# Two decode attention blocks on one core: who issues the loads of x, and how the last cast is split

## The chip, the cores and the metric

The kernel runs on one core of a Trainium2 chip. A core has a matrix engine (TensorE, PE in the profile), two engines for elementwise work (VectorE, DVE; ScalarE, ACT), GpSimd (POOL) and SyncE (SP), which here only issues DMAs. Sixteen DMA engines move data between HBM and the core's SBUF; SyncE and ScalarE each issue into a queue of their own (q1 and q10 in the profile), and both queues run on the same sixteen engines. Engines run side by side and wait for each other and for DMAs by semaphores. TensorE's results land in PSUM, from which VectorE or ScalarE copies them. The metric is device time in microseconds (us) of one execution; the profile's span is the part of it between the first and the last event of the program's engines and DMAs.

## The reference

Two independent problems, A and B, of the same shape; their outputs are put side by side. Each is one decoding step of attention with 2 batches, 32 query heads, 16 key and value heads and a window of the last 4096 positions:

```python
q = (x @ wq).reshape(B, Sq, Hq, Dh)            # x: 2 x 1 x 576, wq: 576 x 4096
k = repeat(k_cache[:, :, Sk - W:, :], 2)       # W = 4096, Dh = 128
v = repeat(v_cache[:, :, Sk - W:, :], 2)
scores = einsum("bhqd,bhkd->bhqk", q, k) * Dh ** -0.5
o = einsum("bhqk,bhkd->bhqd", softmax(scores), v)
out = o.reshape(B, Sq, Hq * Dh) @ wo           # wo: 4096 x 576, out: 2 x 1 x 576
```

Everything is bfloat16. x is tiny (2 rows of 576 numbers, 1152 bytes a row), the weights and above all the cache windows are large: 153 MB are read in all.

## The kernel before, in words

The kernel first builds lists of operations, one list for each engine, in `_Sched` (`S.add(engine, function, dependencies, name)`), and then emits each list in its order with the semaphore waits that the dependencies need. `dma_op` adds a DMA issue to an engine's list. What stands earlier in an engine's list is issued earlier.

**The stream.** Large loads go through a ring of four slots of 4 MB each (`ring`). The list `stream` fixes their order: the query weights of A and of B ("Q"), then K and V windows of the slabs in turn, 16 slabs in all (8 for each problem, each of four key/value heads). SyncE issues them all. A load into a slot waits until the last reader of the slot's previous content is done (`reader`); for a K slab this is VectorE's transpose, for a V slab the matmul with the probabilities, for the query weights the last query matmul. `issue_slab` issues one slab, `issue_wq` the query weights of one problem: first the last 64 of the 576 rows, as 128 half rows of 4 KB (`wqr`, 512 KB), then the other 512 rows (4 MB) into a ring slot. The output weights wo go into a buffer `wob` of their own, in four parts placed between the slabs; the last problem's very last heads come in three small DMAs at the end of the stream (`issue_last`).

**The start.** `load_x` loads x of one problem: a DMA of two rows into `x_sb`. In the kernel before, x of A is the first thing that ScalarE's list holds, and x of B is issued by SyncE at the end of `issue_wq` for A, behind the 4 MB. VectorE meanwhile builds masks (`init_small`), then copies the tail of x (line 380, which waits for both x). TensorE transposes x with five small matmuls (line 375), ScalarE and VectorE cast the result into `xT` (lines 389 and 397), and the query projection begins (`do_qpair`, lines 450 and 188, the second being the helper that reuses loaded weights). It waits for `xT`, the 4 MB of its problem and the half rows of both problems. ScalarE takes the queries out of PSUM (lines 465 and 470), VectorE transposes them (475), ScalarE stores them (483).

**The loop.** For each slab VectorE transposes K in four pieces (line 515), TensorE computes scores (540), VectorE finds maxima (550), ScalarE exponentiates (585), VectorE transposes the probabilities (593), TensorE multiplies with V (631), ScalarE takes the result out (643), and GpSimd, TensorE and VectorE combine it. Groups of heads are then multiplied with wo (`do_proj`, line 786).

**The end.** The output has 576 columns, more than one PSUM bank of 512 float32 numbers. Through most of the kernel the first 512 columns sum up in the bank `OT` and the other 64 apart. Before the last heads, the sums of B are moved into two places of the scores' PSUM tensor, one in each of two banks, that `fin(0)` and `fin(1)` name: ScalarE copies columns 0 to `NH` (line 810), VectorE then adds the 64 (811) and copies the rest (813). The last heads' matmuls add to both (line 790), and `do_E` casts the two to the output row, ScalarE the first (822) and VectorE the second (823). SyncE then issues the output's DMA (831). `NH` is half of 576.

Of the kernel before, what the change touches and what calls it, by code (L numbers as in the profile page):

```python
# [8 lines left out]
ALU = mybir.AluOpType  # L9
# [50 lines left out]
def build_kernel(nc, probs, out, cfg=None):  # L60
# [8 lines left out]
    NPROB = len(probs)  # L69
    Bb, _one, D = x0.shape  # L70
# [12 lines left out]
    ND = SPP * NPROB  # L83
# [5 lines left out]
    HH = HD // 2  # L89
    NXC = NFC + 2  # L90
    NOUT = wo0.shape[1]
    NH = NOUT // 2
    NB0 = 512
    NB1 = NOUT - NB0
    assert NOUT % 2 == 0 and 0 < NB1 <= NB0
    SCALE = float(Dh) ** -0.5
    ZW = 152
    BIG = -1.0e30
# [8 lines left out]
    def by_group(G):  # L107
        return G < NG - 1

    def wo_slot(G):  # L110
        return {0: 0, 1: 8, 2: 16, 3: 24, 4: 0, 5: 8, 6: 16, 7: 24}[G]

    es = ExitStack()
    with es:
# [3 lines left out]
        wob = sb("wob", [128, NSW, NOUT], BF16)  # L118
# [46 lines left out]
        o_rest = sb("o_rest", [Bb, NB1], FP32)  # L165
# [6 lines left out]
        ST = [ps("st%d" % i, [128, 1024]) for i in range(2)]  # L172
# [13 lines left out]
        def matmul_again(e, first, out_ap, rhs, start, stop, skip=True):  # L186
            i = first.ins
            return e.add_instruction(mybir.InstMatmult(  # L188
                name=nc.get_next_instruction_name(), engine=i.engine, ins=[e.lower_ap(rhs), i.ins[1]], outs=[e.lower_ap(out_ap)],
                start_tensor_calc=start, stop_tensor_calc=stop, tile_size=i.tile_size, tile_position=i.tile_position,  # L190
                bass_skip_group_check=skip, ldweights=False))
# [4 lines left out]
        def dma_op(eng, sem_h, n_dmas, fn, deps, tag):  # L196
            op = S.add(eng, fn, deps, tag)
            dma_count[sem_h] = dma_count.get(sem_h, 0) + 16 * n_dmas
            op.dma = (sem_h, dma_count[sem_h])
            return op  # L200

        def load_x(P, eng):
            return dma_op(eng, x_sem, 1, lambda e: e.dma_start(
                x_sb[P * Bb:(P + 1) * Bb, :], probs[P][0][:, 0, :]).then_inc(x_sem, 16), [], "xload%d" % P)
        x_dma = {0: load_x(0, "act")}

        p_ones_b = S.add("pool", lambda e: e.memset(ones_b[:], 1.0), [], "ones_b")
        p_ident_b = S.add("pool", lambda e: e.affine_select(ident_b[:], ones_b[:], [[-1, 128]], ALU.is_equal, 0.0,
# [50 lines left out]
        def issue_wq(n, P):  # L259
            wqP = probs[P][3]  # L260
            r = n % NR
            deps = [reader[n - NR]] if n >= NR else []
            wq_dma[P] = dma_op("sp", wq_sem, 1, lambda e: e.dma_start(
                wqr[:, P, :], wqP[NFC * 128:D, :].rearrange("r (h n) -> r h n", h=2)).then_inc(wq_sem, 16), [], "wqr%d" % P)
            slab_dma[n] = dma_op("sp", ring_sem[r], 1, lambda e: e.dma_start(
                ring[:, r, :], wqP[0:NFC * 128, :].rearrange("(p s) n -> p (s n)", s=NFC)).then_inc(ring_sem[r], 16), deps, "wq%d" % P)

            if P == 0:
                for P_ in range(1, NPROB):
                    x_dma[P_] = load_x(P_, "sp")  # L270

        def issue_last(woP, lo, r0, deps):
            for n_, hs in enumerate(HEADS):
# [51 lines left out]
        rest_add = {}  # L325
# [7 lines left out]
        def tb_job(fn, tag, deps, which=None):  # L333
            n = tbn[0]
            tbn[0] += 1
            w = (tb_last[0] + 1) % NTB if which is None else which
            tb_last[0] = w
            bank = TB[w]
            d = list(deps)
            if tb_open[w] is not None:  # L340
                d.append(tb_open[w]())
            tb_open[w] = lambda: tb_consumer[n]
            return n, bank, S.add("pe", lambda e: fn(e, bank), d, tag)
# [417 lines left out]
        fin_ops = []  # L761

        def fin(half):
            return ST[(ND - 2) % 2][32 * half:32 * half + Bb, 512 * half:512 * half + NH]

        def do_proj(D_):
            G = D_ // 2
            P = G // GPP
            u = unit_of[G]
            s0 = 8 * (G - UNITS[u][0])  # L770
            w0 = wo_slot(G)
            new = G % GPP == 0
            if by_group(G):
                parts = [([(Rsb[u % 2][:, :, s0 + s_], s_) for s_ in range(8)], [r_ev[u], wo_dma[G]], new, True, True)]
            elif D_ < ND - 1:
                parts = [([(Rsb[u % 2][:, :, s_], s_) for s_ in range(4)], [r_ev[u], wo_dma[G]] + fin_ops, False, False, False)]
            else:
                parts = [([(oTn[:, h, :], 4 + h) for h in hs], [norm[D_], wo_last[n_]], False, False, n_ == len(HEADS) - 1)
                         for n_, hs in enumerate(HEADS)]
            for lhs, deps, start, rstart, rstop in parts:  # L780
                def f(e, rest, lhs=lhs, start=start, rstart=rstart, rstop=rstop):
                    last = None
                    for n_, (l_, s_) in enumerate(lhs):
                        begin, end = n_ == 0, n_ == len(lhs) - 1
                        if by_group(G):
                            first = e.matmul(OT[0:Bb, 0:NB0], l_, wob[:, w0 + s_, 0:NB0], start=start and begin, stop=end, skip_group_check=True)  # L786
                            last = matmul_again(e, first, rest[0:Bb, 0:NB1], wob[:, w0 + s_, NB0:NOUT], rstart and begin, rstop and end)
                        else:
                            for half in range(2):
                                last = e.matmul(fin(half), l_, wob[:, w0 + s_, half * NH:(half + 1) * NH],  # L790
                                                start=False, stop=end, skip_group_check=True)
                    return last
                deps = deps + [e_ops[(P - 1, 0)]]
                if by_group(G):
                    n, bank, proj[D_] = tb_job(f, "proj%d" % D_, deps)
                    rest_at[G] = bank
                    if G % GPP < GPP - 1 and G < NG - 2:
                        d = [proj[D_]]
                        if new:
                            if P:  # L800
                                d.append(e_ops[(P - 1, 1)])
                            rest_add[G] = S.add("dve", lambda e: e.tensor_copy(o_rest[:, :], bank[0:Bb, 0:NB1]), d, "rest%d" % G)
                        else:
                            d.append(rest_add[G - 1])
                            rest_add[G] = S.add("dve", lambda e: e.tensor_tensor(o_rest[:, :], o_rest[:, :], bank[0:Bb, 0:NB1], ALU.add),
                                                d, "rest%d" % G)
                        tb_consumer[n] = rest_add[G]
                    elif G == NG - 2:
                        d = [proj[D_], chain[(ND - 2, "exp")], chain[(ND - 2, "max")]]
                        a_ = S.add("act", lambda e: e.activation(fin(0), OT[0:Bb, 0:NH], ACTF.Copy), d, "fin0")  # L810
                        tb_consumer[n] = S.add("dve", lambda e: e.tensor_tensor(
                            fin(1)[:, NB0 - NH:NH], o_rest[:, :], bank[0:Bb, 0:NB1], ALU.add), d + [rest_add[G - 1]], "fin1")
                        fin_ops.append(S.add("dve", lambda e: e.tensor_copy(fin(1)[:, 0:NB0 - NH], OT[0:Bb, NH:NB0]), [a_], "fin2"))
                    else:
                        rest_at[G] = (n, bank)
                else:
                    proj[D_] = S.add("pe", lambda e, f=f: f(e, None), deps, "proj%d" % D_)

        def do_E(P):
            G = (P + 1) * GPP - 1  # L820
            if G == NG - 1:
                e_ops[(P, 0)] = S.add("act", lambda e: e.activation(out_sb[P][:, 0:NH], fin(0), ACTF.Copy), [proj[2 * G + 1]], "Elo%d" % P)
                e_ops[(P, 1)] = S.add("dve", lambda e: e.tensor_copy(out_sb[P][:, NH:NOUT], fin(1)), [proj[2 * G + 1]], "Ehi%d" % P)
# [25 lines left out]
        for s in range(ND):  # L849
# [31 lines left out]
            if s in proj_at:  # L881
                do_proj(2 * proj_at[s] + 1)
                if proj_at[s] == GPP - 1:
                    do_E(0)
# [20 lines left out]
        do_comb(D_)  # L905
        do_norm(D_)
        do_proj(2 * 5 + 1)
        do_redist(2)
        do_comb(ND - 2)
        do_norm(ND - 2)  # L910
        do_proj(D_)
        D_ = ND - 1
        issue_until(len(stream) - 1)
# [78 lines left out]
def bass_concat_heads__sliding_block_cached__sliding_block_cached__decode_kernel(  # L992
    nc, A_x, A_k_cache, A_v_cache, A_wq, A_wo, B_x, B_k_cache, B_v_cache, B_wq, B_wo, out,
):
    build_kernel(nc, [(A_x, A_k_cache, A_v_cache, A_wq, A_wo), (B_x, B_k_cache, B_v_cache, B_wq, B_wo)], out)
# [28 lines left out]
```

## Time and profile before

| what | before |
|---|---|
| device time, median of 3 runs | 362.7 us (362.63 to 363.06) |
| the profiled execution | 363.02 us |
| its span | 361.8 us |
| moved by DMA | 153.27 MB, mean 424 GB/s |
| TensorE, VectorE, ScalarE, GpSimd busy | 60%, 56%, 19%, 10% of the span |
| VectorE transposes of K (line 515) | 64 times, 2284 ns each, 145.3 us |
| last cast, ScalarE / VectorE | 0.400 / 0.449 us |

The profile comes from one execution; its engine rows give start, duration, engine, line, operation and what it wrote from what it read. A bracket at the end of a row gives the engine's idle time before it and what ended that idle time. A row with SPq or ACTq is a DMA issue: its duration is that of the issuing, not of the transfer. "To landing" is the time from issue to the semaphore update that says all data is there. The chain of waits goes back from the last event to what released it, step by step.

### The profile page before, as it was taken

To read this page: it belongs to the slowest core of one execution; us is meant where nothing else is said; L and a number is where in the kernel's file an instruction comes from. 1 tells how busy PE (TensorE), PEld (TensorE's weight loads), DVE (VectorE), ACT (ScalarE), POOL (GpSimd) and SP (SyncE) were. 2 spreads that over 40 slices of the span, in tenths; PEclk is the share of its full clock that TensorE was granted. 3 is DMA by queue.
4 is the path that set the end of the run, shared out by engine and by line. 5 is a ranking of instruction groups with operands and counts; after the bars stand their busy time and mean duration, and the time that the engine had idled before them with its cause. 6 is when DMAs were issued, how large, how long until landed. Compare 5 with 4: busy or idle time off the path is not lost.

```text
span 361.8 us, 2730 instructions
## 1 busy us (share of the span) xinstructions
PE 218.6 (60%) x1318; PEld 55.8 (15%) x945; DVE 200.9 (56%) x175; ACT 68.2 (19%) x149; POOL 35.3 (10%) x55
## 2 busy tenths in 40 slices
PE   0399195763747207466574737766867707657786
PEld 0010021120111101112120201212121201211132
DVE  4112599846647019283756658392919239079931
ACT  1036502130203002103020203020201203002131
POOL 1000000004000400001300040002100040200020
PEclk9999689997889857969698978899898978969999
DMA  8999999999999999999999999999999999999996
GB/s 348 421 449 406 464 406 437 431 408 453 415 442 438 428 424 438 429 428 438 417 446 422 435 428 442 426 435 428 424 424 440 431 424 433 431 438 428 438 409 248
DMA packets 6491, 153.27 MB, mean 424 GB/s; under 512 B 712, under 2 KB 1232, under 8 KB 1616
## 3 DMA queue, kind: packets, MB, share of 16 engines
q1 hardware_dynamic: 6476, 153.10, 98.8%
q8 instruction: 9, 0.15, 0.2%
q14 instruction: 2, 0.02, 0.0%
q10 hardware_dynamic: 4, 0.00, 0.0%
HBM read 153.10 MB, written 0.00 MB: 423 GB/s over the span
## 4 chain that ended last, share of the span: by engine, by line
DMA 72%; DVE 17%; PE 7%; ACT 3%; SPq 1%; issue 0%
DMA ring<-in_B_k_cache_dram 34%; DMA ring<-in_A_k_cache_dram 27%; DVE xt L515 14%; DMA wob<-in_B_wo_dram 8%; DMA wob<-in_B_x_dram 3%; PE st L188 3%; PE st L540 3%; ACT wob L465 1%; DVE wob L475 1%; ACT qk L483 1%; PE st L450 1%; DVE m L550 1%; ACT wob L470 1%; DVE nM L563 0%; SPq L252 0%
## 5 line engine op out<-in xcount | busy, mean ns | idle before, releaser
L515 DVE STREAM_TRANSPOSE xt<-ring 128x2048 f32<-128x2048 f32 x64 | 145.3, 2284 | 86.6 <-DMA ring<-in_A_k_cache_dram 49.8
L540 PE MATMUL st<-xt,zq 128*128 128x512 bf16 x256 | 111.6, 436 | 122.6 <-DVE xt L515 98.1
L188 PE MATMUL st<-xt,zq 128*128 128x512 bf16 x256 | 110.1, 430 | 0.0
L540 PEld LDWEIGHTS st<-xt,zq 128*128 128x128 bf16 x256 | 27.1, 106 | 216.3 <-DVE xt L515 113.5
L631 PE MATMUL acc<-ring,pC 128*32 128x512 bf16 x512 | 32.5, 381 | 1.2 <-DMA ring<-in_B_v_cache_dram 1.2
L568 ACT ACTIVATE nMrep<-nM 1x128 f32<-1x128 f32 x16 | 4.9, 308 | 146.9 <-DVE nM L563 146.9
L643 ACT ACTIVATE acc_sb<-acc 128x512 bf16<-128x512 f32 x16 | 9.5, 596 | 79.9 <-PE acc L631 79.9
L593 DVE STREAM_TRANSPOSE pC<-pR 128x1024 bf16<-128x1024 bf16 x16 | 19.6, 1223 | 3.7 <-ACT pR L585 2.1
L650 POOL TENSOR_TENSOR acc_sb<-acc_sb,masks 128x1024 bf16<-128x1024 bf16 (+1 forms) x8 | 13.4, 1679 | 66.6 <-ACT acc_sb L643 66.6
L550 DVE TENSOR_REDUCE m<-st 128x1 f32<-128x1024 f32 x16 | 19.0, 1190 | 1.4 <-PE st L188 1.4
L502 POOL TENSOR_TENSOR zq<-qk,masks 128x128 bf16<-128x128 bf16 x16 | 6.3, 398 | 136.2 <-PE st L188 114.4
L585 ACT ACTIVATE pR<-st,bias_sb 128x1024 bf16<-128x1024 f32 x16 | 17.8, 1114 | 0.5
L475 DVE STREAM_TRANSPOSE wob<-wob 128x512 f32<-128x512 f32 x8 | 5.7, 711 | 20.3 <-ACT wob L465 12.9
L415 ACT ACTIVATE st<-maskB 128x1024 f32<-128x1024 bf16 x16 | 16.5, 1032 | 1.6 <-POOL rsel L600 0.4
L786 PE MATMUL ot<-wob,Rsb 128*2 128x512 bf16 x56 | 15.2, 390 | 0.0
L631 PEld LDWEIGHTS acc<-ring,pC 128*32 128x32 bf16 x512 | 12.4, 96 | 15.9 <-issue 3.2
L600 POOL TENSOR_TENSOR rsel<-masks,rsum 128x16 f32<-128x16 bf16 x8 | 1.7, 216 | 108.0 <-ACT pR L585 108.0
L188 PE MATMUL tb<-wob,Rsb 128*2 128x64 bf16 x56 | 10.9, 195 | 0.0
L375 PE MATMUL tb<-wob 4*128 4x16 bf16 x5 | 0.3, 179 | 14.5 <-DVE wob L380 14.5
L653 POOL TENSOR_TENSOR acc_sb<-acc_sb 128x512 bf16<-128x512 bf16 (+1 forms) x8 | 8.2, 1029 | 0.6
L188 PE MATMUL st<-ring,wob 128*128 128x512 bf16 x24 | 7.9, 445 | 0.0
L579 ACT ACTIVATE bias_sb<-tb 128x1 f32<-128x1 f32 x16 | 2.7, 171 | 24.8 <-PE tb L573 24.8
(89 smaller groups left out, 99.5 us busy)
## 6 DMA issues: line engine op xcount, KB each, us to landing
ring<-in_A_k_cache_dram SPq DMA_DIRECT2D x8, 4096.0 KB, 30.4
ring<-in_A_v_cache_dram SPq DMA_DIRECT2D x8, 4096.0 KB, 32.5
ring<-in_B_k_cache_dram SPq DMA_DIRECT2D x8, 4096.0 KB, 28.4
ring<-in_B_v_cache_dram SPq DMA_DIRECT2D x7, 4096.0 KB, 32.8
wob<-in_A_wo_dram SPq DMA_DIRECT2D x1, 4608.0 KB, 43.3
ring<-in_A_wq_dram SPq DMA_DIRECT2D x1, 4096.0 KB, 12.7
ring<-in_B_wq_dram SPq DMA_DIRECT2D x1, 4096.0 KB, 22.6
ring<-in_B_v_cache_dram SPq DMA_DIRECT2D x1, 3072.0 KB, 25.5
```

The lines of the kernel that those rows point to most:

```text
L188: return e.add_instruction(mybir.InstMatmult(name=nc.get_next_instruction_name(), engine=i.engine, ins=[e.lower_ap(rhs), i.ins[1]], outs=[ ...
L415: chain[(s, "fill")] = S.add("act", lambda e: e.activation(ST[s % 2][:, :].rearrange("k (h j) -> k h j", h=2), maskB[:].unsqueeze(1).broad ...
L475: chain[(G, "qtr")] = S.add("dve", lambda e: e.transpose(qtr[:].bitcast(FP32), qrow[:].bitcast(FP32)), evs, "qtr%d" % G)
L515: Xop[(s, u)] = S.add("dve", lambda e: e.transpose(xt[:, i % NKT, :].rearrange("k (j w) -> k j w", w=64), ring[:, n % NR, :].bitcast(FP32) ...
L540: first = last = e.matmul(bank, zq[:, p4, s % NZQ, w0:w0 + 128], mv, start=False, stop=stop, skip_group_check=True)
L550: chain[(s, "max")] = S.add("dve", lambda e: e.tensor_reduce(m1[:, 0:1], ST[s % 2][:, :], AX.X, ALU.max), d, "max%d" % s)
L585: chain[(s, "exp")] = S.add("act", lambda e: e.activation(pR[:, :], ST[s % 2][:, :], ACTF.Exp, bias=bias_sb[:, 0:1], scale=SCALE, accum_ou ...
L593: chain[(s, "pC")] = S.add("dve", lambda e: e.transpose(pC[:, s % NPT, :, :].rearrange("k j c -> k (j c)"), pR[:, :]), d, "pC%d" % s)
L631: last = e.matmul(ACC[32 * cb:32 * cb + 32, 0:512], pC[:, D_ % NPT, j0_:j0_ + 4, :].rearrange("k j c -> k (j c)"), ring[:, n % NR, j0_ * 1 ...
L643: acc_ev[D_] = S.add("act", lambda e: e.activation(acc_sb[:, D_ % 2, :], ACC[:, :], ACTF.Copy), d, "accev%d" % D_)
L650: t = S.add("pool", lambda e: e.tensor_tensor(v, v, maskJ[:].unsqueeze(1).unsqueeze(3).broadcast_to([128, l1 - l0, 4, 128]), ALU.mult), [a ...
L786: first = e.matmul(OT[0:Bb, 0:NB0], l_, wob[:, w0 + s_, 0:NB0], start=start and begin, stop=end, skip_group_check=True)
```

## The change

Both loads of x are issued by SyncE, between the half rows (`wqr`) of A's query weights and their 4 MB; ScalarE issues none. Independently, `NH` goes from 288 to 320, so that ScalarE copies and casts 320 columns of the last output and VectorE 256; the matmuls of the last heads and the copies that preload `fin(0)` and `fin(1)` follow the new border.

```diff
-    NH = NOUT // 2
+    NH = NOUT * 5 // 9
     NB0 = 512
     NB1 = NOUT - NB0
...
-        x_dma = {0: load_x(0, "act")}
+        x_dma = {}
...
             wq_dma[P] = dma_op("sp", wq_sem, 1, lambda e: e.dma_start(
                 wqr[:, P, :], wqP[NFC * 128:D, :].rearrange("r (h n) -> r h n", h=2)).then_inc(wq_sem, 16), [], "wqr%d" % P)
+            if P == 0:
+                for P_ in range(NPROB):
+                    x_dma[P_] = load_x(P_, "sp")
             slab_dma[n] = dma_op("sp", ring_sem[r], 1, lambda e: e.dma_start(
                 ring[:, r, :], wqP[0:NFC * 128, :].rearrange("(p s) n -> p (s n)", s=NFC)).then_inc(ring_sem[r], 16), deps, "wq%d" % P)
-
-            if P == 0:
-                for P_ in range(1, NPROB):
-                    x_dma[P_] = load_x(P_, "sp")
...
-            return ST[(ND - 2) % 2][32 * half:32 * half + Bb, 512 * half:512 * half + NH]
+            return ST[(ND - 2) % 2][32 * half:32 * half + Bb, 512 * half:512 * half + (NOUT - NH if half else NH)]
...
-                                last = e.matmul(fin(half), l_, wob[:, w0 + s_, half * NH:(half + 1) * NH],
+                                last = e.matmul(fin(half), l_, wob[:, w0 + s_, half * NH:NOUT if half else NH],
...
-                            fin(1)[:, NB0 - NH:NH], o_rest[:, :], bank[0:Bb, 0:NB1], ALU.add), d + [rest_add[G - 1]], "fin1")
+                            fin(1)[:, NB0 - NH:NOUT - NH], o_rest[:, :], bank[0:Bb, 0:NB1], ALU.add), d + [rest_add[G - 1]], "fin1")
```

More of the change, by code (lines that the diff above doesn't have):

```diff
@@ L91, in build_kernel @@
     NOUT = wo0.shape[1]
-    NH = NOUT // 2
+    NH = NOUT * 5 // 9
     NB0 = 512
     NB1 = NOUT - NB0
-    assert NOUT % 2 == 0 and 0 < NB1 <= NB0
+    assert NOUT % 9 == 0 and 0 < NB1 <= NOUT - NH and NH < NB0
     SCALE = float(Dh) ** -0.5
```

## The prediction

> **What bounds the kernel now.** I read three views in this order: the page's slices, to see whether one resource is full throughout; the chain of waits, to see what sets the end; the timeline of the first and last microseconds, since the change touches only those. The slices and the queues come first.
>
> ```profile
> DMA  8999999999999999999999999999999999999996
> GB/s 348 421 449 406 464 406 437 431 408 453 415 442 438 428 424 438 429 428 438 417 446 422 435 428 442 426 435 428 424 424 440 431 424 433 431 438 428 438 409 248
> ...
> q1 hardware_dynamic: 6476, 153.10, 98.8%
> ...
> q10 hardware_dynamic: 4, 0.00, 0.0%
> ```
>
> Every slice but the first and the last has the 16 DMA engines at 90% or more, and SyncE's queue q1 alone fills 98.8% of the span. The kernel streams 153.10 MB and is bound by that stream; its time is the stream's start, plus its bytes, plus what follows the last byte. q10 is ScalarE's queue, with the four packets of x of problem A. The start, in the timeline (columns: start us, duration us, engine, line, what):
>
> ```profile
> 0.79 0.53 ACTq L203 DMA_DIRECT2D wob<-in_A_x_dram  x1
> 0.79 0.40 SPq L263 DMA_DIRECT2D wob<-in_A_wq_dram  x1
> ...
> 1.25 0.41 SPq L265 DMA_DIRECT2D ring<-in_A_wq_dram  x1
> ...
> 1.72 0.31 SPq L203 DMA_DIRECT2D wob<-in_B_x_dram  x1
> ...
> 14.20 0.21 DVE L380 COPY wob<-wob 4x128 bf16<-4x128 bf16 x1 [9.47 <-DMA wob<-in_B_x_dram]
> ...
> 15.42 0.59 PE L450 MATMUL st<-wob 128*128 128x512 bf16 x1 [0.63 <-DVE wob L397]
> ```
>
> VectorE waited 9.47 us for x of problem B, which queued behind 4 MB of wq; that looks like the prize. The end:
>
> ```profile
> 356.87 0.61 PE L631 MATMUL acc<-ring,pC 128*32 128x512 bf16 x8 [1.01 <-DMA ring<-in_B_v_cache_dram]
> ...
> 359.75 0.08 PEld L790 LDWEIGHTS st<-wob,oTn 128*2 128x2 bf16 x2 [0.27 <-DMA wob<-in_B_wo_dram]
> 360.08 0.40 ACT L822 ACTIVATE pR<-st 2x288 bf16<-2x288 f32 x1 [1.88 <-PE st L790]
> 360.08 0.45 DVE L823 CAST pR<-st 2x288 bf16<-2x288 f32 x1 [1.37 <-PE st L790]
> 360.57 0.26 SPq L831 DMA_DIRECT2D out_dram<-pR  x1
> ```
>
> The last wo rows land at 359.71 by the chain; then two matmuls (0.31 us), the two casts side by side, VectorE's the longer, and the output's DMA, with the span's end at 361.8.
>
> **The early x, as a gain.** Both x go out right behind the first wq half rows (512 KB). Those landed 3.5 us after their issue by the view of DMAs, at 4.29, so both x are there by about 4.4 (my estimate: the same landing and two tiny rows). VectorE is busy with masks until 4.72, so x's preparation (copy 0.21, matmuls 0.32, casts 0.22 and 0.19: the rows from 14.20 to 15.28, 1.1 us in all) ends near 5.8 instead of 15.28. The q projection has two other waits. The 4 MB of wq landed at 1.25 + 12.7 = 13.95, and the second problem's half rows, for which every projection also waits, at 2.07 + 13.2 = 15.27. So the first matmul of q moves from 15.42 to about 15.3: 0.1 us, not 9. Of the 9.47 us VectorE's wait loses, all is idle time of an engine off the path; what is late next is the second half rows.
>
> What that 0.1 us is worth: the q matmuls free the first two ring slots, and the next 4 MB loads go out at 26.99 and 36.04. The load of 36.04 took 29.02 us in the chain. 4 MB at the 437 GB/s of most 6 us stretches take 9.6 us, so it lay some 19 us behind earlier transfers. Loads issued 0.1 us earlier start no earlier. Gain: 0, from 0 to 0.1; the backlog of 19 us is the cover.
>
> **The early x, as a cost.** In SyncE's order the 4 MB come two issues later: x issues take 0.31 each on SyncE, with 0.06 between issues, so 2 x 0.37 = 0.74. The 4 MB issue moves from 1.25 to 1.99, the second half rows from 2.07 to 2.44 (one issue more than before), and the second 4 MB and the two K slabs by the same 0.37. Does the stream stall? The windows of a quarter microsecond show when data moves (columns: busy time by engine, then PE's clock, DMA share, GB/s; packets are counted where they start):
>
> ```profile
> 1.50:1.75 0.25, 0.00 (x0) 0.00 (x0) 0.22 (x1) 0.25 (x1) 0.00 (x0) 1.00 0.01 5
> 1.75:2.00 0.25, 0.00 (x0) 0.00 (x0) 0.20 (x1) 0.25 (x1) 0.00 (x0) 1.00 0.94 147
> ...
> 3.00:3.25 0.25, 0.00 (x0) 0.00 (x0) 0.25 (x2) 0.00 (x0) 0.00 (x0) 1.00 1.09 442
> 3.25:3.50 0.25, 0.00 (x0) 0.00 (x0) 0.25 (x2) 0.00 (x0) 0.00 (x0) 1.00 2.29 934
> ```
>
> The half rows, issued at 0.79, start to move at about 1.8: 1.0 us from issue to first packet. The jump to 934 GB/s between 3.25 and 3.50 is the first big packets of the 4 MB. By the same 1.0 us they could have moved from 2.25; they waited some 1.1 us for the 512 KB ahead of them (at 437 GB/s alone 1.2 us). Delayed by 0.74 they are ready near 3.0, still 0.35 us before their turn. Cost: 0, and the half rows are the cover. Without it the 0.74 us would be lost whole, at the stream's head. Other prices for the issue: 0.26 (the last output, SyncE), 0.53 (the same x on ScalarE, the first DMA there) and 1.05 (the other output row of two, at 332.3, into a full queue). At 0.53 the delay is 1.18 and the stall 0.1; at 1.05 it is 2.2 and the stall 1.1. I take 0.31, the same transfer on the same engine 0.5 us away.
>
> In the queue itself the two x are two rows of 1152 bytes each. In the kernel before, one x lay between the 4 MB and the second half rows; these landed 1.32 us apart where 512 KB take 1.2, so one x holds the queue for 0.1 us at most. That one only moves, and the one from q10 comes out of the same 16 engines' time: 0 to 0.1, taken as 0.
>
> The Trainium skill, in "DMA: Bandwidth & Descriptors", section "Anatomy of one DMA — SWDGE (gpsimd) path", gives a DMA on the path it describes (issued by GpSimd, not SyncE) a fixed cost of about 2.0 us. Read as time in which a queue stands still (rival 2 below, in this kernel's own rows), two x would add an estimated 4 us less 1.1 of cover and the sum would be 365.6. The trace speaks against that reading with the 1.32 us above, and the page itself lays most of the cost to completion.
>
> **ScalarE's side.** Its issue of 0.53 goes. Its next work, a table load, ran from 1.36 to 2.64, and then it waited 12.19 us for x: worth nothing there. With nothing issued beside SyncE's first DMA, that one might reach the engines sooner; bound: ScalarE's x took 0.53 where SyncE's took 0.31, so at most 0.2. No row separates the two; I take 0, nearest to SyncE's first issue (0.40), no longer than its second (0.41).
>
> **The last cast.** VectorE goes from 288 to 256 columns. Its copy of 224 columns (line 813) took 0.393, its cast of 288 took 0.449: 0.88 ns a column, so 0.421. ScalarE goes from 288 to 320; 1024 columns took 1.004 and 512 took 0.582 (lines 465 and 470): 0.82 ns a column, so 0.400 + 0.026 = 0.426. SyncE waits for both, so the end moves from 0.449 to 0.426: -0.02 (bounds: 0, if all of ScalarE's 0.400 scaled with width and gave 0.444; -0.03, VectorE's share alone). The casts that preload the sums shift the same 32 columns, +0.03 on ScalarE and then -0.03 on VectorE, ending near 355.04; the matmul stand-ins behind them start at 357.48, a cover of 2.4 us. The matmuls stay at 320 + 256 = 288 + 288 columns a head: 0.
>
> **Sum.** 0 + 0 + 0 - 0.02. The profiled execution took 363.02 (its span 361.8 and 1.2 around it), 0.3 above the median of 362.7; the runs lie between 362.63 and 363.06. The difference taken from the median gives 362.68, say 362.7. About 0.2%, 0.7 us, is what can be told from no change here, more than any term of this sum.
>
> **Rivals.**
> 1. The stream stalls at its head (slower). Place: between the half rows and the 4 MB, 3.0 to 4.0 us. It starts once an x costs SyncE over 0.49 (1.1 / 2 less 0.06), and adds twice the excess. For it: 0.53 and 1.05 among issue rows. Against: SyncE's own x, 0.31. At 1.05 it gives 363.8; it passes 0.2% from 0.86 on. Chance of that 0.09.
> 2. Each small DMA holds the queue from issue to landing instead of overlapping. The first half rows took 3.5 from issue to landing, of which their bytes make 1.2, so 2.3 are fixed; two x in front of the 4 MB would make it late by 4.6 less 1.1 of cover: 366.2. The 1.32 us between two landings with an x between them speak against it: 0.03.
> 3. The start gets shorter (faster): the first DMA sooner by up to 0.2 without ScalarE's beside it, q sooner by 0.1, and the 1.2 us around the span shorter with one queue never used. The first two give 362.4, still within 0.2%. Only the third, which no row shows, passes it: with half of the 1.2 gone, 361.8. Chance 0.13.
> 4. Something not on the list at the tail: engines of the stream that finish at other moments. The instruction queue's nine packets (0.2% of 16 engines' span, 0.7 us) sit in the same engines; one of them falling otherwise costs some tenths. Both signs; 0.03 to the slow side beyond 0.2%.
>
> That it does nothing measurable is the forecast itself, at 0.72; with the rest slower 0.15, faster 0.13. The forecast's own range is 362.3 to 363.1 (the runs' spread, and the bounds of -0.3 and +0.2 above). For eight in ten it reaches half way into rivals 1 and 3: 362.1 to 363.4.
>
> **What would show it.** Right: VectorE's copy at line 380's place starting near 4.8; the first q matmul still near 15.3, now ended by wq's second half rows; the loads after it still taking 28 us or so; the big packets still beginning between 3.25 and 3.50; casts of 0.43 and 0.42 at the end, with the last wo landing near 359.7. Wrong: a window between 2.5 and 4.5 with the DMA share well under 1, the first data before 1.6, or the last wo rows landing over 0.5 us from 359.7.

## The result, and the profile after

| | before | changed |
|---|---|---|
| device time, median of 6 runs | 362.75 us (362.63 to 363.06) | 364.97 us (364.73 to 365.06) |
| ratio to the kernel before | 1 | 1.0059, 95% interval 1.0046 to 1.0072 |
| the profiled execution; its span | 363.02; 361.8 | 364.96; 363.7 |
| 4 MB of A's wq landed | 13.95 | 16.1 |
| first query matmul | 15.42 | 17.52 |
| last wo rows landed | 359.71 | 361.62 |

The kernel became 2.2 us slower. The page's slices and queues of the changed kernel:

```profile
DMA  7999999999999999999999999999999999999995
GB/s 267 432 422 443 422 443 420 443 420 440 425 431 447 418 432 432 431 432 429 436 429 434 425 440 422 441 418 443 422 418 455 418 429 438 425 436 429 434 408 225
...
q1 hardware_dynamic: 6480, 153.10, 98.4%
```

The first slice fell from 8 to 7 tenths and from 348 to 267 GB/s; from the second on the engines are full as before. The first 18 us of the timeline (start us, duration us, engine, line, what):

```profile
0.79 0.39 SPq L263 DMA_DIRECT2D wob<-in_A_wq_dram  x1
...
1.24 0.31 SPq L203 DMA_DIRECT2D wob<-in_A_x_dram  x1
1.60 0.23 SPq L203 DMA_DIRECT2D wob<-in_B_x_dram  x1
...
1.88 0.36 SPq L268 DMA_DIRECT2D ring<-in_A_wq_dram  x1
...
3.22 2.52 SPq L256 DMA_DIRECT2D ring<-in_A_k_cache_dram  x2
...
4.64 0.20 DVE L379 COPY wob<-wob 4x128 bf16<-4x128 bf16 x1
...
17.52 0.59 PE L449 MATMUL st<-wob 128*128 128x512 bf16 x1 [12.29 <-DMA wob<-in_B_wq_dram]
```

x came 9.6 us sooner: VectorE copies it at 4.64 without waiting, where it started at 14.20 before. But the first query matmul starts 2.1 us later, because the half rows of the second problem, behind the 4 MB in the queue, landed later. And the two K issues that stand at 3.22 take 2.52 us together (0.61 and 1.87); before, the same two took 1.26. The windows of a quarter microsecond (DMA share and GB/s are the last two columns; packets are counted where they start) show the hole:

```profile
1.75:2.00 0.25, 0.00 (x0) 0.00 (x0) 0.20 (x1) 0.25 (x1) 0.00 (x0) 1.00 1.01 229
...
3.25:3.50 0.25, 0.00 (x0) 0.00 (x0) 0.25 (x2) 0.00 (x0) 0.00 (x0) 1.00 1.73 566
3.50:3.75 0.25, 0.00 (x0) 0.00 (x0) 0.25 (x2) 0.00 (x0) 0.00 (x0) 1.00 0.38 131
3.75:4.00 0.25, 0.00 (x0) 0.00 (x0) 0.25 (x3) 0.00 (x0) 0.00 (x0) 1.00 0.44 131
4.00:4.25 0.25, 0.00 (x0) 0.00 (x0) 0.25 (x3) 0.00 (x0) 0.00 (x0) 1.00 0.43 131
4.25:4.50 0.25, 0.00 (x0) 0.00 (x0) 0.25 (x3) 0.00 (x0) 0.00 (x0) 1.00 0.00 0
```

In the kernel before, the two K issues of the timeline and the same windows read (the quarter from 3.25, with 934 GB/s, stands in the prediction):

```profile
3.00 1.26 SPq L256 DMA_DIRECT2D ring<-in_A_k_cache_dram  x2
...
3.50:3.75 0.25, 0.00 (x0) 0.00 (x0) 0.25 (x2) 0.00 (x0) 0.00 (x0) 1.00 2.92 1213
...
4.00:4.25 0.25, 0.00 (x0) 0.00 (x0) 0.25 (x3) 0.00 (x0) 0.00 (x0) 1.00 0.00 0
```

The data begins to move in the same quarter as before. But where the 4 MB should set in at once on all engines (934 and 1213 GB/s of packets started in the two quarters from 3.25 before), a few engines begin, then hardly any until 4.5. A row of zero alone is no hole: before, nothing starts from 4.00 to 4.50 either, because all sixteen engines are still on the packets that started from 3.37 to 3.92.

From the trace's DMA packets this can be counted in two terms. Idle: between 2 and 6 us the sixteen engines stood idle for 1.00 us on average, before 0.07. Slow packets: a 32 KB packet takes 1.215 us as a rule; in the first 20 us the packets took longer than that by 0.91 us in all, divided by 16 engines, before 0.11. The two terms grew by 1.73 us together, most of the 1.9 by which the span grew. From 11 us on, until the stream runs out, both are as before: the next 4 MB landed at 27.1 instead of 25.0, the K slabs behind them at 36.9 and 46.6 instead of 34.7 and 44.4, always 2.1 to 2.2 later. The stream, full to its end, carries the loss to the last byte. The two terms are means over the engines, and the last packet goes by the engine that finishes last: from 340 us to the last packet the engines were idle for 3.37 us on average, before 2.83. What follows the last byte is as short as before:

```profile
361.66 0.08 PEld L789 LDWEIGHTS st<-wob,oTn 128*2 128x2 bf16 x2 [0.28 <-DMA wob<-in_B_wo_dram]
362.00 0.43 ACT L821 ACTIVATE pR<-st 2x320 bf16<-2x320 f32 x1 [1.85 <-PE st L789]
362.00 0.41 DVE L822 CAST pR<-st 2x256 bf16<-2x256 f32 x1 [1.34 <-PE st L789]
362.52 0.26 SPq L830 DMA_DIRECT2D out_dram<-pR  x1
```

The casts take 0.43 and 0.41 instead of 0.40 and 0.45.

### The profile page after: what moved, and what is told of

It is laid out like the page before. It is cut to its first block, busy times and chain, and to the rows that moved or that the text cites. A ratio compares the mean times of both kernels' runs of the same rounds, so it can differ in the third digit from the quotient of the medians.

```text
span 363.7 us, 2728 instructions
## 1 busy us (share of the span) xinstructions
PE 221.6 (61%) x1316; PEld 56.2 (15%) x945; DVE 200.6 (55%) x175; ACT 68.3 (19%) x149; POOL 35.3 (10%) x55
## 4 chain that ended last, share of the span: by engine, by line
DMA 72%; DVE 17%; PE 6%; ACT 3%; SPq 1%; issue 0%
DMA ring<-in_B_k_cache_dram 33%; DMA ring<-in_A_k_cache_dram 27%; DVE xt L514 15%; DMA wob<-in_B_wo_dram 8%; DMA wob<-in_B_wq_dram 4%; PE st L188 3%; PE st L539 2%; ACT wob L464 1%; DVE wob L474 1%; DVE m L549 1%; ACT qk L482 1%; PE st L449 1%; ACT wob L469 1%; DVE nM L562 0%; SPq L252 0%
## 5 line engine op out<-in xcount | busy, mean ns | idle before, releaser
L539 PEld LDWEIGHTS st<-xt,zq 128*128 128x128 bf16 x256 | 27.1, 106 | 213.8 <-DVE xt L514 109.9
L785 PE MATMUL ot<-wob,Rsb 128*2 128x512 bf16 x56 | 16.9, 420 | 0.0
L449 PE MATMUL st<-wob 128*128 128x512 bf16 x4 | 2.0, 494 | 12.3 <-DMA wob<-in_B_wq_dram 12.3
```

The source lines that it names most:

```text
L539: first = last = e.matmul(bank, zq[:, p4, s % NZQ, w0:w0 + 128], mv, start=False, stop=stop, skip_group_check=True)
```

## The experiments

The question was why 0.63 us of lateness in one DMA issue costs over 2 us. The theories as they came up: **T**, a tiny transfer holds up what is issued behind it on its queue; **L**, the lateness of the 4 MB itself; **A**, ScalarE's missing issue; and, after the first results, **M**, the moment at which the 4 MB are issued. The kernel before was run beside each group and had medians between 362.84 and 362.97 us; every ratio below is to the kernel before of the same group.

### The x loads alone, a delay alone, one x, and both x behind

x_only keeps the changed kernel but splits the cast as before:

```diff
-    NH = NOUT * 5 // 9
+    NH = NOUT // 2
```

> The changed kernel with the last cast split 288 and 288 as before: only the loads of x are moved. Every theory here puts the whole loss at the start, so 365.0 us (within 0.1 of the changed kernel). If the cast had a part in the loss, it would come out below 364.5.

Measured 365.01 us (364.14 to 365.84), ratio 1.0055 (1.0036 to 1.0073). The loss is in the x loads. The four executions lie 1.7 us apart, and the profiled one is the fastest, 364.14: the same issues at the same times as in the changed kernel, but the two K issues take 1.99.

delay_only is the kernel before with one wait more ahead of the 4 MB:

```diff
-            deps = [reader[n - NR]] if n >= NR else []
+            deps = [reader[n - NR]] if n >= NR else [p_zxT] if P == 0 else []
```

> The kernel before, x where it was, but SyncE waits ahead of the 4 MB of A's wq until VectorE's clearing of xT is done (1.72 us), so that the 4 MB are issued near 1.8 as in the changed kernel (1.88), with no DMA in between. Theory L (lateness: the 4 MB of descriptors take long to be made, and issued 0.6 later they no longer get ahead of the engines): 364.2 to 365.0, packets of the 4 MB starting one engine after another up to about 5.3, K issues of over 1.2 us each. Theory T (tiny transfers: a DMA of two rows holds up what is issued behind it on the same queue by about 1 us each): 362.7 to 363.1, at most the 0.3 by which the issue comes later than its cover.

Measured 365.47 us (365.37 to 365.69), ratio 1.0068 (1.0051 to 1.0085). SyncE's issues in its timeline:

```profile
0.80 0.40 SPq L263 DMA_DIRECT2D wob<-in_A_wq_dram  x1
1.76 0.35 SPq L265 DMA_DIRECT2D ring<-in_A_wq_dram  x1
2.16 0.32 SPq L203 DMA_DIRECT2D wob<-in_B_x_dram  x1
2.52 0.34 SPq L263 DMA_DIRECT2D wob<-in_B_wq_dram  x1
2.91 0.43 SPq L265 DMA_DIRECT2D ring<-in_B_wq_dram  x1
3.38 2.53 SPq L256 DMA_DIRECT2D ring<-in_A_k_cache_dram  x2
```

Nothing stands between the half rows and the 4 MB but 0.5 us of waiting, and the loss is there in full, with the slow K issues (2.53 for two, 1.37 and 1.12). That removes theory T as the cause. It also shows that the cost is far more than the lateness. The two terms of above explain only part of it here: idle (0.59) and slow packets (0.96) grew by 1.37 us together, of 2.5 in the profiled execution. Another 1.36 stands at the stream's end, where from 340 us to the last packet the engines were idle for 4.19 us on average against 2.83 before. So the engines finish at more different moments. That some engines were held up more than others at the start would explain it, but the trace doesn't say which engine ran a packet, and so this is not shown.

one_x leaves A's x to ScalarE and puts B's x alone ahead of the 4 MB:

```diff
+            if P == 0:
+                x_dma[1] = load_x(1, "sp")
             slab_dma[n] = dma_op("sp", ring_sem[r], 1, lambda e: e.dma_start(
...
-            if P == 0:
-                for P_ in range(1, NPROB):
-                    x_dma[P_] = load_x(P_, "sp")
```

> x of A by ScalarE as before; x of B alone in front of the 4 MB on SyncE's queue. The 4 MB go out near 1.6. Theory T: about half the loss, 363.6 to 364.0. Theory L: only the 0.35 us of lateness, 363.0 to 364.0 by how steep the loss is, and no more than delay_only. Theory A (what costs is that ScalarE no longer issues its x at the very start): 362.7.

Measured 364.21 us, ratio 1.0032 (1.0017 to 1.0048), with the 4 MB issued at 1.60. The executions lie anywhere between 362.98 and 365.11: at this moment it sometimes costs next to nothing and sometimes all.

sp_behind has both x on SyncE's queue behind the 4 MB, none by ScalarE:

```diff
-        x_dma = {0: load_x(0, "act")}
+        x_dma = {}
...
-                for P_ in range(1, NPROB):
+                for P_ in range(NPROB):
```

> Both x by SyncE, none by ScalarE, but both behind the 4 MB of A's wq. The 4 MB go out at 1.25 as before. Theory A: 365. Theory L: 362.7. Theory T: 362.7 to 363.2 (the two tiny transfers now hold up the second half rows, with 4 MB ahead as cover).

Measured 362.81 us (362.72 to 362.84), ratio 0.9995 (0.9986 to 1.0004): no loss. Theory A falls, and x by SyncE is harmless as long as the 4 MB go first.

### More delay, more cover, the 4 MB first, and x by ScalarE

delay_more is delay_only with `p_zq` in place of `p_zxT`.

> The kernel before with SyncE waiting ahead of the 4 MB of wq until VectorE has cleared zq (2.36 us), so that the 4 MB go out at about 2.4 instead of 1.25. Waiting until 1.76 cost 2.5 us. If the cost grows with each moment of lateness as it did there (2.5 for 0.51, so 4.9 for each us late): 368. If running late switches the start into a poorer course with a price of its own of about 2, to which only the further lateness adds: 366.0 to 366.3. If the stream simply had to start its 4 MB a fixed time after the issue: 1.15 late less the 1.1 of cover, 362.9, which delay_only has already spoken against.

Measured 364.04 us (363.83 to 364.15), ratio 1.0031 (1.0019 to 1.0043). None of the three forecasts has this: issued 0.63 later than in delay_only, the 4 MB cost 1.4 us less. Lateness alone can't be the cause.

cover issues the half rows of both problems, then both x, then the 4 MB:

```diff
+            if P == 0:
+                for P_ in range(NPROB):
+                    wq_dma[P_] = dma_op("sp", wq_sem, 1, lambda e, P_=P_: e.dma_start(
+                        wqr[:, P_, :], probs[P_][3][NFC * 128:D, :].rearrange("r (h n) -> r h n", h=2)).then_inc(wq_sem, 16), [], "wqr%d" % P_)
+                for P_ in range(NPROB):
+                    x_dma[P_] = load_x(P_, "sp")
```

> Both x by SyncE ahead of the 4 MB as in the changed kernel, but behind the half rows of both problems: 512 KB, 512 KB, x, x, 4 MB, 4 MB. The 4 MB go out some 2.4 us into the span, later than in any kernel so far, but with 1 MB instead of 512 KB ahead of them (1.2 us more of cover). Theory L with cover: 362.7 to 363.2. Theory T (what holds the queue is the tiny transfer itself): 364.5 to 365. If the issue time alone counts, whatever lies ahead: 366.

Measured 363.92 us (363.35 to 364.06), ratio 1.0025 (1.0015 to 1.0035), a miss for theory L: the 4 MB went out at 2.37 and were not due before 4.6, as much ahead as in the kernel before (3.37 - 1.25), and still 1.0 us was lost. The engines idled for only 0.20 us here; slow packets took 0.70.

big_first issues the 4 MB ahead of the half rows (the two statements change places).

> The 4 MB of wq first of all, then the 512 KB of half rows; x as in the kernel before. Nothing lies ahead of the 4 MB, so the first packet of each DMA engine shows when its first descriptor was ready. Theory L: the engines begin one after another over 1 to 2 us, where behind the 512 KB of half rows they begin within 0.5; time 364 to 365.5, the cover being gone. If making the descriptors is quick: all engines begin within 0.5 us and the time is 362.7.

Measured 363.46 us, ratio 1.0038 (1.0015 to 1.0060), in two groups: five executions between 363.18 and 363.60, three between 365.33 and 365.70. In the profiled one, of the first group, the sixteen engines began within 0.8 us, from 1.83 to 2.60, and their first packets were slow, 0.75 us over the rule on average. So 4 MB with nothing ahead of them aren't taken up one engine after another over several microseconds. What the second group met isn't in a profile.

both_act gives both x to ScalarE:

```diff
-        x_dma = {0: load_x(0, "act")}
+        x_dma = {P_: load_x(P_, "act") for P_ in range(NPROB)}
```

> Both x by ScalarE at the very start, none by SyncE, which issues the 4 MB at 1.25 as before: x comes early without the 4 MB coming late. Theory L and theory T: 362.5 to 362.8, since an early x brings the first query matmul forward by 0.1 us only and nothing waits for that.

Measured 362.88 us (362.67 to 363.60), ratio 1.0001 (0.9992 to 1.0010). x is there at 4.9, the 4 MB go out at 1.26, and nothing is gained or lost. From its timeline:

```profile
15.31 0.59 PE L446 MATMUL st<-wob 128*128 128x512 bf16 x1 [10.09 <-DMA wob<-in_B_wq_dram]
```

That is the first query matmul at 15.3, ended by the second half rows, as the prediction had it for an early x.

### The moment

delay_little waits for `p_ident_b` and delay_long for `p_ident_f` in delay_only's place.

> The kernel before with SyncE waiting ahead of the 4 MB until GpSimd has the bfloat16 identity (1.36 us), so that the 4 MB go out near 1.4 instead of 1.25, 0.15 late. Theory L (lateness against the 512 KB ahead): 362.7 to 363.2, still within the cover. If the poorer course begins with any lateness: 364 to 365.5 in part of the runs.

Measured 362.90 us (362.65 to 363.61), ratio 1.0003 (0.9994 to 1.0012).

> The same, waiting for GpSimd's float32 identity (2.86 us), so that the 4 MB go out near 2.9, 1.65 late. The engines then run dry before the 4 MB are there: first big packets near 4.0 where 3.4 is their turn. 1.76 cost 2.5 us and 2.39 cost 1.1. If what is dear is making the 4 MB's descriptors while the half rows run, and a late issue only costs its lateness: 364.0 to 364.8, growing by the 0.5 from delay_more. If lateness as such is dear: 366 and more.

Measured 364.05 us (363.92 to 364.22), ratio 1.0035 (1.0021 to 1.0049). Between 1.76 and 2.39 the cost falls, and from 2.39 to 2.89 it stays.

big_first_late is big_first with the 4 MB waiting for `p_zxT`, alone at 1.76.

> The 4 MB of wq first of all, with nothing ahead of them, but issued only near 1.8, when VectorE has cleared xT; the half rows and x behind. big_first was 363.5 in the median with its issue at 0.79. If what is dear is the 4 MB being prepared while the 512 KB run, this costs its lateness of 1.0 alone: 364.2 to 364.7. If an issue near 1.8 is dear by its moment (something else at the start that runs beside it): 366 and more.

Measured 364.12 us (363.90 to 364.49), ratio 1.0038 (1.0024 to 1.0051). That is just below the lower forecast of 364.2 to 364.7: issued at 1.76 with nothing ahead, 0.96 us later than in big_first, the 4 MB cost 0.7 us more than its median, no more than their lateness. So, as far as four executions show, 1.76 is dear only with the half rows starting up at that time.

sp_behind_cast is the changed kernel with its loop over both x moved behind the 4 MB.

> Both x by SyncE behind the 4 MB, none by ScalarE, with the cast of 320 and 256 columns: the changed kernel with the x loads at a harmless place. All theories: 362.6 to 362.9, the time of the kernel before or up to 0.2 less, of which the cast gives 0.02 to 0.04.

Measured 362.89 us (362.76 to 363.48), ratio 1.0003 (0.9994 to 1.0012). With the x loads at a harmless place, the changed cast can't be told from the old one.

Theory M says: the half rows' first packet moves about 1.0 us after their issue began. If the issue of the 4 MB has ended by then, they follow at full speed; if it runs or begins just while the engines start on the half rows, they are taken up slowly; later they cost less again. Three kernels were made to tell it from the others. after_wait makes the changed kernel wait longer:

```diff
-            deps = [reader[n - NR]] if n >= NR else []
+            deps = [reader[n - NR]] if n >= NR else [p_zq] if P == 0 else []
```

> The changed kernel, with SyncE waiting a little longer ahead of the 4 MB, until VectorE has cleared zq (2.36 us): the same DMAs in the same order, the 4 MB at 2.4 instead of 1.88. Theory M (the moment: a large DMA is taken up slowly when it is issued while the engines are starting on the one ahead of it, from about 1.6 to 2.2 us; later it costs only its lateness): faster than the changed kernel by 1, at 363.9 to 364.2, and K issues of 0.6 to 0.75 us instead of 1.26. Theory L (lateness) or theory T (tiny transfers): 365.0 to 365.6, no faster than the changed kernel.

Measured 363.94 us (363.64 to 364.25), ratio 1.0028 (1.0018 to 1.0038), against 1.0059 (1.0046 to 1.0072) of the changed kernel. From its timeline:

```profile
0.80 0.40 SPq L263 DMA_DIRECT2D wob<-in_A_wq_dram  x1
1.25 0.31 SPq L203 DMA_DIRECT2D wob<-in_A_x_dram  x1
1.62 0.23 SPq L203 DMA_DIRECT2D wob<-in_B_x_dram  x1
2.40 0.36 SPq L268 DMA_DIRECT2D ring<-in_A_wq_dram  x1
...
3.74 1.25 SPq L256 DMA_DIRECT2D ring<-in_A_k_cache_dram  x2
```

A wait of 0.5 us added to the changed kernel made it 1.0 us faster, and the two K issues take 1.25 again. Neither lateness nor the tiny transfers explain that.

shift holds back the half rows until `p_zxT`, with the 4 MB right behind them.

> The kernel before with its whole start 1.0 us later: the half rows wait until 1.72 and the 4 MB follow 0.45 behind them, at about 2.2, issued before the engines start on the half rows near 2.8. Theory M: only the lateness, 363.6 to 363.9. If the time from the span's start is what counts: 365 or more, as at 1.76.

Measured 363.86 us (363.83 to 364.39), ratio 1.0030 (1.0018 to 1.0042): 1.0 us of lateness cost 1.0 us, although the 4 MB went out at 2.20.

x_first puts both x ahead of the half rows:

```diff
-        x_dma = {}
+        x_dma = {P_: load_x(P_, "sp") for P_ in range(NPROB)}
...
-            if P == 0:
-                for P_ in range(NPROB):
-                    x_dma[P_] = load_x(P_, "sp")
```

> Both x first of all on SyncE's queue, then the half rows (near 1.5) and the 4 MB (near 1.95). Only the half rows' lateness of 0.7 should count by theory M, as the 4 MB follow 0.45 behind them and ahead of their start: 363.3 to 363.7. By theory T, 365 as in the changed kernel. If the engines' very first transfer of any size sets the moment (the x would start near 1.8): 365.

Measured 363.50 us (363.42 to 363.64), ratio 1.0014 (1.0005 to 1.0024). From its timeline:

```profile
0.79 0.34 SPq L203 DMA_DIRECT2D wob<-in_A_x_dram  x1
1.19 0.24 SPq L203 DMA_DIRECT2D wob<-in_B_x_dram  x1
1.48 0.36 SPq L263 DMA_DIRECT2D wob<-in_A_wq_dram  x1
1.89 0.42 SPq L265 DMA_DIRECT2D ring<-in_A_wq_dram  x1
...
3.30 1.26 SPq L256 DMA_DIRECT2D ring<-in_A_k_cache_dram  x2
```

The same SyncE issues as in the changed kernel, the same 4 MB at the same 1.9, but with the half rows 0.4 ahead of them and not 1.1: the cost is 0.6, about the 0.7 by which the stream's head comes later.

All runs with 512 KB of half rows right ahead of the 4 MB or with x between, by the distance of the two issues (idle: engine time lost between 2 and 6 us; slow: 32 KB packets of the first 20 us over 1.215 us; both in us for each of 16 engines, from the packets of the one profiled execution, whose own time stands beside the median of all):

| run | half rows, 4 MB issued at | distance | median | profiled one | idle | slow | two K issues |
|---|---|---|---|---|---|---|---|
| x_first | 1.48, 1.89 | 0.41 | 363.50 | 363.56 | 0.58 | 0.11 | 1.26 |
| shift | 1.75, 2.20 | 0.45 | 363.86 | 363.84 | 0.93 | 0.09 | 1.25 |
| sp_behind | 0.80, 1.25 | 0.45 | 362.81 | 362.81 | 0.12 | 0.06 | 1.26 |
| before | 0.79, 1.25 | 0.46 | 362.75 | 363.02 | 0.07 | 0.11 | 1.26 |
| sp_behind_cast | 0.80, 1.26 | 0.46 | 362.89 | 362.78 | 0.16 | 0.11 | 1.27 |
| both_act | 0.79, 1.26 | 0.47 | 362.88 | 362.71 | 0.07 | 0.06 | 1.26 |
| delay_little | 0.79, 1.39 | 0.60 | 362.90 | 362.66 | 0.03 | 0.15 | 1.25 |
| one_x | 0.80, 1.60 | 0.80 | 364.21 | 363.55 | 0.14 | 0.54 | 1.66 |
| delay_only | 0.80, 1.76 | 0.96 | 365.47 | 365.56 | 0.59 | 0.96 | 2.53 |
| changed | 0.79, 1.88 | 1.09 | 364.97 | 364.96 | 1.00 | 0.91 | 2.52 |
| x_only | 0.79, 1.88 | 1.09 | 365.01 | 364.14 | 0.67 | 0.50 | 1.99 |
| delay_more | 0.79, 2.39 | 1.60 | 364.04 | 364.05 | 0.57 | 0.56 | 1.48 |
| after_wait | 0.80, 2.40 | 1.60 | 363.94 | 364.06 | 0.48 | 0.77 | 1.25 |
| delay_long | 0.79, 2.89 | 2.10 | 364.05 | 364.04 | 0.61 | 0.75 | 1.27 |

Up to 0.6 the slow packets are at most 0.15, and what idle time there is comes from a late head. In all these runs the issue of the 4 MB had ended before the half rows' first packet moved (delay_little at 1.74 and 1.82). At 0.8 to 1.1, with the first half-row packets moving at 1.0, the slow packets rise, from 0.96 on the idle time too, and the issues behind back up; how much, differs between executions (x_only and the changed kernel have the same issues at the same times). From 1.6 on 0.6 to 0.8 of slow packets stays, with the lateness. cover fits these last rows (2.37 for the 4 MB, engines long running, slow 0.70), which is why its longer cover didn't save it.

The packets show what stays there. In after_wait and delay_long each engine's first 32 KB packet took 1.5 to 2.3 us, and the later ones 1.22; up to a distance of 0.6 the first ones took 1.2 to 1.5. big_first has the same slow first packets with nothing ahead. So part of what an early issue of the 4 MB saves is this slow first packet.

What stays open is what happens inside: why an issue that falls into that half microsecond is taken up slowly, why first packets are slow, and why the same issues cost 1.2 us in one execution of x_only and 2.9 in another. The records show when packets run and how long issues take, and nothing of what lies between. The slower group of big_first isn't explained by M either: there the 4 MB have nothing ahead of them.

## Why the prediction was wrong

**What held.** x early is worth nothing: x was ready by 5.7 us (5.8 was worked out). Where it came early without disturbing the 4 MB, in both_act, the first query matmul moved from 15.42 to 15.31 and the time stayed. The backlog that covers the later loads is there in every run: K loads of A took 30 to 32 us from issue to landing, by the median of each run. The cast went from 0.449 to 0.43 (0.426 was worked out), with 0.41 for VectorE (0.421), too little to measure. The x issues were no dearer than taken, 0.31 and 0.23, and the 4 MB went out at 1.88 where 1.99 was forecast. Leaving ScalarE's queue empty changed nothing (sp_behind, 362.81 with a span of 361.5), which disposes of rival 3.

**The step that failed** is in "The early x, as a cost": "Delayed by 0.74 they are ready near 3.0, still 0.35 us before their turn. Cost: 0". It took the 1.0 us from the issue to the first packet of the very first DMA, on idle engines, for the time that any DMA needs, and it took "the first packet is there" for "all sixteen engines can run". In the changed kernel the first big packets did start at 3.24, close to the 3.0 and in their turn. But only seven packets had started by 4.7, all still running, so nine of sixteen engines had got none 2.8 us after the issue; and packets that started up to about 8 us were slow. The missing price was 2.2 us by the medians (1.9 by the spans of the two profiled executions) in place of 0. Of the 1.9, the growth of idle time is 0.93 and that of slow packets 0.80.

**The rival that came nearest** was the first, a stall at the stream's head, with the right place (3.0 to 4.0 us, and on to 4.5) and the right consequence (the stream carries it to the end). Its condition was wrong. It asked for an x that costs over 0.49 on SyncE; it cost at most 0.31, and the stall came all the same, and comes without any x in delay_only. Its price at the far bound was 1.1; rightly it was 2.2. So even as a rival, the stall was priced by a simple sum of issue times, where the runs show a step of about 2 us that depends on the moment.

Rival 2 fell: with both x ahead of the stream's head, x_first lost 0.6 us, not 4. With it fell the strict reading of the fixed cost that the Trainium skill gives in "DMA: Bandwidth & Descriptors", section "Anatomy of one DMA — SWDGE (gpsimd) path", for DMAs that GpSimd issues. The Trainium skill, in "DMA: Bandwidth & Descriptors", section "Issuing engines are not separate DMA queues", says that issuing from several engines only saves the sequencer's time, usually small beside the transfer. Here that small time, 0.63 us of SyncE's, stood at the one place where it was worth 2 us; the trace has 0.31 and 0.23 for the issues. both_act, with x issued by ScalarE, took 362.88, and x_only, with x issued by SyncE, 365.01.

The view that could have warned was in the profile of before: in the timeline the 4 MB's issue ends at 1.66 and the half rows' first packets start in the window from 1.75. The kernel before has its second large DMA issued just ahead of the engines' start, and the change moved it across that line. But no row of that profile has a large DMA issued on the other side with only the half rows ahead, so the price could not be read there; a far wider bound was due for an issue moved across it. One of the prediction's signs of being wrong, a window between 2.5 and 4.5 with the DMA share well under 1, could not have told: the kernel before has 0.00 from 4.00 to 4.50. Its other sign, the last wo rows over 0.5 us from 359.7, came true with 361.62.

## What to carry to other kernels

In a kernel bound by one DMA stream, issue the first large transfers back to back, ahead of everything small, and let tiny loads follow behind them or go out from another engine: in these runs a tiny load's place among the first issues decided over up to 2.2 us, and how early its data came over nothing. A cover worked out from when a transfer is due and how long one issue took to its first packet failed twice here, in the changed kernel and in cover; for the first microseconds of a stream, try the order on the chip. And when an unexplained loss looks like lateness, add more of it: here half a microsecond more made the kernel 1.0 us faster, which told the moment from the delay.

## What the runs showed that was not expected

- A 4 MB DMA issued 0.8 to 1.1 us after the 512 KB ahead of it, while the engines start on those, lost 1.2 to 2.5 us by the medians; issued 0.4 to 0.6 us after it, nothing beyond the lateness of the 512 KB; 1.6 to 2.1 us after it, 1.0 to 1.2.
- While the engines take up the 4 MB slowly, SyncE's next issues can take twice or three times as long: 0.61 and 1.87 us for the two K slabs in the changed kernel, 1.37 and 1.12 in delay_only, instead of 0.62 and 0.60.
- 4 MB issued first on idle engines (big_first) started on all sixteen within 0.8 us, but the first 32 KB packets took about 0.75 us longer on average than the 1.215 of later ones.
- 4 MB due 2.2 us after their issue, but issued while the engines were already running on 1 MB of half rows (cover), still lost 0.7 us to slow packets.
